# Exchange transfers that write eight spread partitions, bulk loads on the GpSimd queue, and a tile for each exchanged array

## The chip, the cores and the metric

One core of one Trainium2 chip runs the whole program. The metric is the device time of one execution in microseconds (us). The engines of the core are TensorE (PE in the profile, with its weight loads as PEld), VectorE (DVE), ScalarE (ACT), GpSimd (POOL) and SyncE (SP). Transfers are issued from the SP, ACT and POOL queues and run on 16 DMA engines.

## The reference

Two layers of a spectral filter and an MLP over an array x of 2048 rows by 576 columns, in bf16. Each layer has these two residual steps:

```
def _A_ref(x, w_r, w_i):                       # 2-D filter over rows and columns
    X = rfft2(x.astype(float32))               # 2048 x 289 complex
    return irfft2(X * (w_r + 1j * w_i), s=(S, D)).astype(bfloat16)

def _B_ref(x, w1, b1, w2, b2):                 # MLP, 576 -> 4608 -> 576
    y = _layernorm(x)
    h = _gelu(einsum("bsd,df->bsf", y, w1) + b1)
    return einsum("bsf,fd->bsd", h, w2) + b2

x = x + _A_ref(_layernorm(x), w_r, w_i);  x = x + _B_ref(_layernorm(x), ...)   # twice
```

## The kernel before, in words

x stays in SBUF as 16 tiles of 128 rows (x_sb). The Fourier transforms are matrix products on TensorE. The transform along the 2048 rows is split into a step of 16 and a step of 128, and between the two the data must change partitions. An "exchange" does that: a transfer from SBUF to SBUF, 128 rows of 1160 bytes (145 KB), from the SP queue.

A layer runs through these stages:

- SpectralIn (L250 to L322): for each of 16 tiles t, in the order of E_ORDER, fold and layernorm statistics on DVE (L257, L232 to L248; the inverse square root is three Newton steps on DVE, L244 to L247), transposes and two products on PE (L270 to L298), evacuations on ACT or DVE, and an exchange of tile y1 (three buffers, L299) into vx (L304). In the first layer this runs alone (run_all, L309); in the second layer it is woven into the MLP of the first, and only the last tile stands alone after it.
- middle (L327 to L376): 16 steps, each with four matmuls (dft_u, L340), an ACT copy (L342), four DVE operations with the filter weights (L351 to L354), four matmuls (idft_c, L363), an ACT copy into h (three buffers, L365) and an exchange of h into hx (L366). Every dft_u reads all 128 partitions of vx, so the first one needs all 16 exchanges of SpectralIn.
- spectral_out (L380 to L442): products with hx (L391, L404) and c_gd (L420), residual sums on DVE (L426 to L428), and the layernorm of the first quarter for the MLP (Prep, L444). Its first matmul, L404, needs all 16 exchanges of the middle.
- mlp (L516): four quarters of 4 tiles, mlp_up (L472, 38 us) and mlp_down (L497).

Order. Inside a manual_schedule region (L179) every engine, SP too, issues its instructions in the order of the program text. The SP queue carries the x loads, all exchanges, the loads of the first middle (c_f2, filter weights, i1: each exchange of the first SpectralIn is followed by two of them, L305) and those for the MLP (w1 and small ones: one after each exchange of the first middle, L367). The POOL queue carries the w2 loads (L222) and the middle loads of the second layer (L577), which wait until the last mlp_down has read the hidden activations that lie in the same memory.

Memory. One tile, arena_sb, holds vx or hx, w2, the temporaries of the middle and the hidden activations, at offsets. An exchange writes `dst[8 * slot : 8 * slot + 8]`: eight neighbouring partitions.

Of the kernel before, what the change touches and what calls it, by code (L numbers as in the profile page):

```python
# [29 lines left out]
ENGINES = [getattr(mybir.EngineType, n) for n in ("PE", "Activation", "DVE", "Pool", "SP")]  # L30
# [78 lines left out]
def kernel(  # L109
# [40 lines left out]
    arena_sb = arena.tile([P, (OFF_HT + 36864) // 2], BF16, name="arena_sb")  # L150

    def at(shape, name, off):
        n = int(np.prod(shape[1:]))
# [32 lines left out]
    nc.scalar.dma_start(out=c_k1[:], in_=const_ap("k1"))  # L186
    for b in u2r_buf:
        nc.gpsimd.memset(b[:], 0.0)

# [4 lines left out]

    def middle_loads(wks, i1s, with_f2):
        calls = []
        for j in range(4):
            if with_f2:
                calls.append(lambda eng, j=j: eng.dma_start(out=c_f2[:, j::4], in_=f2_ap[:, j::4]))
            for ri, w_ap in enumerate((A_w_r, A_w_i)):  # L200
                wv = w_ap.rearrange("(c e) k -> c e k", e=16)
# [4 lines left out]
    def mlp_const_loads():
        calls = [
            lambda eng: eng.dma_start(out=c_r1[:], in_=const_ap("r1")),
            lambda eng: eng.dma_start(out=c_gd[:], in_=const_ap("gd")),
            lambda eng: eng.dma_start(out=b1_rows[:], in_=B_b1.rearrange("(fc p) -> fc p", p=128)),  # L210
            lambda eng: eng.dma_start(out=b2_bc[:], in_=B_b2.partition_broadcast(P)),
        ]
        for ci in range(4):
            calls.append(lambda eng, ci=ci: eng.dma_start(out=w1_sb[:, ci, :], in_=B_w1[ci * 128 : (ci + 1) * 128, :]))
# [4 lines left out]

    def load_w2(w2s, groups):  # L220
        for g in groups:
            nc.gpsimd.dma_start(  # L222
                out=w2s[g][:], in_=B_w2[g * 768 : (g + 1) * 768, :].rearrange("(fc p) d -> p fc d", p=128)
            )

    def ln_stats(tiles, mlp):
# [100 lines left out]
    def middle(li, vx, hx, wks, i1s, loads):  # L327
        off = OFF_W2 + 18592
        m = {}
        for nm in ("xs", "ma", "mb", "xp"):  # L330
            m[nm] = [(off + 1184 * (len(m) * 2 + b)) for b in range(2)]
        m["h"] = [off + 1184 * (8 + b) for b in range(3)]
        st = {}

        def dft_u(n):
# [180 lines left out]
    def mlp(li, w2s, prep, spec):  # L516
        prev = None
        last = li == N_LAYERS - 1
        for q in range(4):
# [3 lines left out]
            for i, t in enumerate(QUADS[q]):  # L523
# [24 lines left out]

    vx = at([P, 16, 2, KP], "vx", OFF_W2)
    hx = at([P, 16, 2, KP], "hx", OFF_B)  # L550
    wks, i1s = middle_tiles(0)
    for wk in wks:
        nc.gpsimd.memset(wk[:, :, :, KP - 1 : KP], 0.0)
    SpectralIn(vx, middle_loads(wks, i1s, True)).run_all()

    for li in range(N_LAYERS):
        last = li == N_LAYERS - 1
# [8 lines left out]
        spectral_out(hx, prep)
        load_w2(w2s, (0, 1, 2))
        if last:
            mlp(li, w2s, prep, None)
        else:  # L570
            vx = at([P, 16, 2, KP], "vx", OFF_B)
            mlp(li, w2s, prep, SpectralIn(vx))
            hx = at([P, 16, 2, KP], "hx", OFF_W2)
            wks, i1s = middle_tiles(li + 1)
            for wk in wks:
                nc.gpsimd.memset(wk[:, :, :, KP - 1 : KP], 0.0)
            for call in middle_loads(wks, i1s, False):  # L577
                call(nc.gpsimd)
# [30 lines left out]
```

## Time and profile before

| | |
|---|---|
| median of 6 runs | 905.94 us (903.46 to 908.84) |
| the profiled execution's own time | 903.79 us |
| its span, first to last instruction | 902.0 us |
| PE busy | 772.1 us (86%) |
| ACT busy | 330.7 us (37%) |
| DVE busy | 289.3 us (32%) |
| POOL busy | 20.7 us (2%) |
| on the chain that ended last: PE, DMA, DVE | 71%, 16%, 7% |
| moved by DMA | 41.60 MB, mean 46 GB/s |

The shares are means over stages with different limits. The stages, by the start of their first matmul in the trace, are: SpectralIn 1 to 83.2 us, middle 1 to 150.1, spectral_out 1 to 185.5, MLP 1 with SpectralIn 2 to 509 (the end of the last y1 evacuation), a gap to 520.6, middle 2 to 570.3, spectral_out 2 to 605.5, MLP 2 to the end.

### The profile page before, as it was taken

The numbers are of one execution on the slowest core, as the hardware profiler recorded it, in microseconds if no ns is written. First come the engines' busy times: TensorE is split into PE (matmuls) and PEld (weight loads), VectorE is DVE, ScalarE is ACT, GpSimd is POOL, SyncE is SP. The second block draws the span as 40 slices with busy tenths as digits, with TensorE's granted clock in tenths as the row PEclk, the third lists the DMA queues.
The fourth block names the chain that finished last, engine by engine and source line by source line (L and its number), as shares of the span: only waits on it lengthen the run. The fifth ranks groups of instructions, "written<-read, shape, count | busy, mean of one in ns | idle before, by whom it ended". The sixth has DMA issues, their size and how long they took to land.

```text
span 902.0 us, 12359 instructions
## 1 busy us (share of the span) xinstructions
PE 772.1 (86%) x5121; PEld 471.1 (52%) x5121; DVE 289.3 (32%) x989; ACT 330.7 (37%) x506; POOL 20.7 (2%) x38
## 2 busy tenths in 40 slices
PE   5765434799999999999999364689999999999998
PEld 3443222544863684487368232453684485386366
DVE  6632421960442245034014253493013014011001
ACT  3444322356225424632642143336404513521620
POOL 0000001000000000000000400010000000000000
PEclk9997755899999999999999786789999999999999
DMA  6973985300000000000000945330000000000000
GB/s 180 172 132 42 174 158 115 117 0 1 8 14 1 7 15 8 1 14 15 1 7 14 217 51 55 91 118 1 7 15 7 1 15 14 1 14 15 1 7 21
DMA packets 29001, 41.60 MB, mean 46 GB/s; under 512 B 4144, under 2 KB 25072, under 8 KB 28432
## 3 DMA queue, kind: packets, MB, share of 16 engines
q1 hardware_dynamic: 24960, 25.78, 16.3%
q0 software_dynamic: 3584, 14.56, 5.4%
q8 instruction: 40, 0.66, 0.3%
q10 hardware_dynamic: 400, 0.47, 0.2%
q14 instruction: 17, 0.14, 0.1%
HBM read 28.93 MB, written 2.36 MB: 35 GB/s over the span
## 4 chain that ended last, share of the span: by engine, by line
PE 71%; DMA 16%; DVE 7%; ACT 2%; issue 1%; ACTq 0%; DVEq 0%
DMA arena_sb<-arena_sb 11%; DVE tt L426 2%; DMA arena_sb<-y_413 1%; DMA arena_sb<-y_539 1%; DMA arena_sb<-y_4639 1%; DVE x_sb L427 1%; PE psb_4090 L504 1%; PE psb_3278 L504 1%; PE psb_2466 L504 1%; PE psb_7434 L504 1%; PE psb_6818 L504 1%; PE psb_6202 L504 1%; PE psb_5586 L504 1%; PE psb_1704 L504 1%; PE psb_4468 L504 1%
## 5 line engine op out<-in xcount | busy, mean ns | idle before, releaser
L504 PEld LDWEIGHTS <-arena_sb 128*128 128x128 bf16 x2304 | 223.2, 98 | 58.3 <-issue 3.4
L478 PEld LDWEIGHTS <-w_sb 128*128 128x128 bf16 x1152 | 107.3, 98 | 148.7 <-issue 28.1
L456 DVE TENSOR_SCALAR xn<-x_sb,mv,rs 128x576 bf16<-128x576 bf16 x32 | 13.6, 426 | 194.9 <-PE pss_6291 L466 33.8
L232 DVE BATCH_NORM_STATS2 stats<-x_sb 128x6 f32<-128x288 bf16 x128 | 50.4, 436 | 0.0
L340 PEld LDWEIGHTS <-c_f_75 128*128 128x128 bf16 x128 | 15.4, 122 | 64.1 <-issue 45.4
L351 DVE TENSOR_TENSOR arena_sb<-arena_sb 128x580 bf16<-128x580 bf16 x32 | 14.7, 459 | 67.8 <-ACT arena_sb L342 56.7
L280 PEld LDWEIGHTS <-xT 96*128 96x128 bf16 x192 | 21.9, 118 | 14.2 <-ACT xT L272 4.9
L270 PEld LDWEIGHTS <-xf 128*96 128x96 bf16 x192 | 19.2, 159 | 18.0 <-DVE xf L257 16.5
L484 PEld LDWEIGHTS <-w1r_sb 64*128 64x128 bf16 x288 | 8.2, 94 | 30.5 <-issue 30.5
L500 DVE TENSOR_TENSOR xb<-x_sb,b_bc 128x576 f32<-128x576 bf16 x32 | 24.0, 749 | 0.0
L363 PEld LDWEIGHTS <-arena_sb 128*128 128x128 bf16 x128 | 14.3, 119 | 17.4 <-DVE arena_sb L353 6.8
L404 PEld LDWEIGHTS <-arena_sb 128*34 128x34 bf16 x128 | 4.3, 108 | 25.8 <-DMA arena_sb<-arena_sb 24.7
L390 PEld LDWEIGHTS <-arena_sb 128*128 128x128 bf16 x128 | 14.1, 117 | 4.3 <-issue 0.4
L246 DVE TENSOR_TENSOR tt<-tt,hv 128x1 f32<-128x1 f32 (+1 forms) x93 | 14.9, 161 | 3.2
L247 DVE SCALAR_TENSOR_TENSOR rs<-tt,rs 128x1 f32<-128x1 f32 (+1 forms) x93 | 14.9, 160 | 3.2
L245 DVE TENSOR_TENSOR tt<-rs 128x1 f32<-128x1 f32 (+1 forms) x93 | 14.9, 160 | 3.2
L222 POOL DMA_DIRECT2D arena_sb<-in_B_w_dram x12 | 10.0, 840 | 239.6 <-DMA arena_sb<-arena_sb 212.0
L512 DVE TENSOR_TENSOR x_sb<-psb_7434,xb 128x576 bf16<-128x576 f32 x1 | 0.8, 758 | 44.3 <-PE psb_7434 L504 44.3
L352 DVE TENSOR_TENSOR arena_sb<-arena_sb 128x580 bf16<-128x580 bf16 x32 | 14.5, 454 | 0.0
L512 DVE TENSOR_TENSOR x_sb<-psb_4090,xb 128x576 bf16<-128x576 f32 x1 | 0.8, 757 | 42.3 <-PE psb_4090 L504 42.3
L233 DVE BATCH_NORM_AGGREGATE mv<-stats 128x2 f32<-128x12 f32 x64 | 13.4, 209 | 2.2
L466 PEld LDWEIGHTS <-xn 128*128 128x128 bf16 x160 | 11.8, 100 | 3.1 <-DVE xn L456 1.6
(1228 smaller groups left out, 1412.0 us busy)
## 6 DMA issues: line engine op xcount, KB each, us to landing
arena_sb<-in_B_w_dram POOLq DMA_DIRECT2D x12, 864.0 KB, 7.2
arena_sb<-arena_sb SPq DMA_DIRECT2D x32, 145.0 KB
w_sb<-in_B_w_dram SPq DMA_DIRECT2D x4, 1152.0 KB
x_sb<-in_A_x_dram SPq DMA_DIRECT2D x4, 576.0 KB
out_dram<-x_sb SPq DMA_DIRECT2D x16, 144.0 KB
c_f_75<-const_f SPq DMA_DIRECT2D x4, 384.0 KB
arena_sb<-const_i SPq DMA_DIRECT2D x4, 384.0 KB
arena_sb<-const_i POOLq DMA_DIRECT2D x4, 384.0 KB, 9.0
```

Source lines behind the costliest of these rows:

```text
L232: nc.vector.bn_stats(out=stats[:, h, :], in_=x_sb[:, t, h * DH : (h + 1) * DH])
L245: nc.vector.tensor_mul(out=tt[:], in0=rs[:], in1=rs[:])
L246: nc.vector.tensor_mul(out=tt[:], in0=tt[:], in1=hv[:])
L247: nc.vector.scalar_tensor_tensor(out=rs[:], in0=tt[:], scalar=1.5, in1=rs[:], op0=ALU.add, op1=ALU.mult)
L270: nc.tensor.transpose(pt[0:96, 3 * o + ci, :], xf[:, o, 96 * ci : 96 * ci + 96], ident[:])
L280: nc.tensor.matmul(pz[:, o, 0:KP], lhsT=xT[:, 3 * o + ci, :], rhs=c_fd[:, 3 * o + ci, :], start=(ci == 0), stop=(ci == 2),)
L340: nc.tensor.matmul(px[:, o, 0:KP], lhsT=c_f2[:, e, pl, :], rhs=vx[:, e, ri, :], start=(q == 0), stop=(q == 1))
L351: nc.vector.tensor_mul(out=ma[:], in0=xs[:], in1=wr)
L426: nc.vector.tensor_tensor(out=tt[:], in0=po[:, 0:1, 0:DH].to_broadcast([P, 2, DH]), in1=xr, op=ALU.add)
L478: nc.tensor.matmul(phs[q // 2][:, q % 2, :], lhsT=w1_sb[:, ci, (fg + q) * 128 : (fg + q + 1) * 128], rhs=yT[:, ci, :], start=(ci == 0), st ...
L500: nc.vector.tensor_tensor(out=xb[:], in0=xr, in1=b2_bc[:].rearrange("p (h n) -> p h n", h=2), op=ALU.add)
L504: nc.tensor.matmul(po[:, h, 0:DH], lhsT=hts[fc][:, i * 128 : (i + 1) * 128], rhs=w2s[fc // 6][:, fc % 6, h * DH : (h + 1) * DH], start=(fc ...
```

## The change

- An exchange into slot s writes partitions p0, p0+4, ..., p0+28, with p0 = 32 (s // 4) + s % 4, where it wrote 8s to 8s+7. The rows of two constant matrices (f2, r1) are permuted on the host to match (SLOT_ROWS).
- For each pair of exchanges into the same array any ordering that the framework would draw between them is taken away (declare_no_dep).
- SP is no longer among the engines that keep the program's order.
- Bulk loads go to the POOL queue and are issued at the start: three quarters of x, the constants and filter weights of the first middle, then those for the MLP with w1. SP keeps the four first tiles of x, the exchanges and the output.
- arena_sb is cut into v_sb and b_sb (vx and hx by turns), r_sb (temporaries of the middle) and h_sb (hidden activations, or filter weights and i1). w2 comes in 4 parts of 8, 8, 10 and 10 chunks, in v_sb and r_sb, where it came in 6 parts of 6. In layer 1 all four are issued behind the middle; in layer 2 parts 2 and 3 behind the middle and parts 0 and 1 behind spectral_out.
- h has four buffers instead of three.
- In the first SpectralIn and the first Prep the inverse square root is one ACT Sqrt and one DVE reciprocal.
- Two memsets (u2r_buf) move from POOL to DVE.

The core of the diff:

```diff
-ENGINES = [getattr(mybir.EngineType, n) for n in ("PE", "Activation", "DVE", "Pool", "SP")]
+SLOT_ROWS = [8 * (4 * (p // 32) + p % 4) + (p // 4) % 8 for p in range(128)]
+ENGINES = [getattr(mybir.EngineType, n) for n in ("PE", "Activation", "DVE", "Pool")]
...
-    arena_sb = arena.tile([P, (OFF_HT + 36864) // 2], BF16, name="arena_sb")
+    v_sb = arena.tile([P, 9296], BF16, name="v_sb")
+    b_sb = arena.tile([P, 9296], BF16, name="b_sb")
+    r_sb = arena.tile([P, 20 * D], BF16, name="r_sb")
+    h_sb = arena.tile([P, NFC * 512], BF16, name="h_sb")
...
-    for j in range(4):
-        nc.sync.dma_start(out=x_sb[:, j::4, :], in_=xv[:, j::4, :])
+    for t in QUADS[0]:
+        nc.sync.dma_start(out=x_sb[:, t, :], in_=xv[:, t, :])
...
-        nc.gpsimd.memset(b[:], 0.0)
+        nc.vector.memset(b[:], 0.0)
+    for j in range(1, 4):
+        nc.gpsimd.dma_start(out=x_sb[:, j::4, :], in_=xv[:, j::4, :])
...
+    w2_parts = [at(v_sb, [P, 8, D]), at(v_sb, [P, 8, D], 8 * D), at(r_sb, [P, 10, D]), at(r_sb, [P, 10, D], 10 * D)]
+    w2_first = (0, 8, 16, 26, 36)
...
+        if sqrt:
+            sq = work.tile([P, n], F32, tag="ln_v")
+            nc.scalar.activation(out=sq[:], in_=mv[:, :, 1], func=ACT.Sqrt, ...)
+            nc.vector.reciprocal(out=rs[:], in_=sq[:])
+            return [(mv[:, i, 0:1], rs[:, i : i + 1]) for i in range(n)]
...
-            exchange(self.vx, t, y1)
-            for call in self.loads[:2]:
-                call(nc.sync)
-            self.loads = self.loads[2:]
+            exchange(self.vx, t, y1[:])
...
     def exchange(dst, slot, src):
-        nc.sync.dma_start(out=dst[8 * slot : 8 * slot + 8], in_=src[:])
+        p0 = 32 * (slot // 4) + slot % 4
+        ins = nc.sync.dma_start(out=dst[p0 : p0 + 29 : 4], in_=src).ins
+        before = exchanged.setdefault(id(dst), [])
+        for b in before:
+            tc.declare_no_dep(ins, b, query=mybir.DependencyQuery.ANY_SYNC, reason="other partitions of the array")
+        before.append(ins)
...
-            h = at([P, 2, KP], f"h{li}", m["h"][n % 3])
+            h = at(r_sb, [P, 2, KP], 592 * (8 + n % 4))
             nc.scalar.copy(out=h[:], in_=ph[:, :, 0:KP])
             exchange(hx, E_ORDER[n], h)
-            if loads:
-                loads.pop(0)(nc.sync)
...
-    SpectralIn(vx, middle_loads(wks, i1s, True)).run_all()
+    middle_loads(wks, i1s, True)
+    mlp_const_loads()
+    SpectralIn(vx, sqrt=True).run_all()
...
-        load_w2(w2s, (5, 4, 3))
-        prep = Prep(0)
         if li == 0:
+            load_w2((0, 1, 2, 3))
...
+        else:
+            load_w2((2, 3))
+        prep = Prep(0, sqrt=li == 0)
         spectral_out(hx, prep)
-        load_w2(w2s, (0, 1, 2))
         if last:
-            mlp(li, w2s, prep, None)
+            load_w2((0, 1))
+            mlp(li, prep, None)
```

## Rows read from the trace of the kernel before

**Rows 1.** The page's slices: 40 equal parts of the span, DMA busy tenths and GB/s.
```profile
DMA  6973985300000000000000945330000000000000
GB/s 180 172 132 42 174 158 115 117 0 1 8 14 1 7 15 8 1 14 15 1 7 14 217 51 55 91 118 1 7 15 7 1 15 14 1 14 15 1 7 21
```

**Rows 2.** Windows: stretch, length, busy us by engine; PE clock, DMA share, GB/s.
```profile
0.00:10.00 10.00, 1.84 (x11) 1.26 (x12) 2.78 (x14) 2.08 (x2) 2.23 (x11) 1.00 0.80 247
...
186.00:225.00 39.00, 38.36 (x195) 15.56 (x193) 10.17 (x37) 22.62 (x37) 0.00 (x0) 1.00 0.00 1
...
497.00:509.00 12.00, 7.78 (x58) 5.31 (x56) 4.03 (x18) 3.36 (x5) 9.72 (x13) 0.89 0.91 206
509.00:514.00 5.00, 0.00 (x0) 0.00 (x0) 0.00 (x0) 0.55 (x1) 0.00 (x0) 0.50 1.01 289
...
528.00:562.00 34.00, 18.77 (x92) 10.57 (x90) 16.19 (x49) 13.60 (x23) 0.00 (x0) 0.73 0.56 56
```

**Rows 3.** Waits of all engines: who waited for whom, us in total, times, longest.
```profile
ACT arena_sb L365 <- DMA arena_sb<-arena_sb: 58.0, 25, 5.9
```

**Rows 4.** Timeline, borders of the middles: start, us, instruction, idle before.
```profile
83.21 1.12 PE L340 MATMUL psb_763<-arena_sb,c_f_75 128*128 128x290 bf16 x4 [7.35 <-DMA arena_sb<-y_760]
...
150.07 1.04 PE L404 MATMUL pss_1051<-c_r_76,arena_sb 128*34 128x128 bf16 x16 [11.95 <-DMA arena_sb<-arena_sb]
...
509.58 0.61 SPq L325 DMA_DIRECT2D arena_sb<-y_4639  x1
520.64 1.15 PE L340 MATMUL psb_4658<-arena_sb,c_f_75 128*128 128x290 bf16 x4 [11.77 <-DMA arena_sb<-y_4639]
521.59 1.17 PE L340 MATMUL psb_4668<-arena_sb,c_f_75 128*128 128x290 bf16 x4
...
525.25 39.55 SPq L325 DMA_DIRECT2D arena_sb<-arena_sb  x16
...
570.26 1.04 PE L404 MATMUL pss_4933<-c_r_76,arena_sb 128*34 128x128 bf16 x16 [12.12 <-DMA arena_sb<-arena_sb]
```

**Rows 5.** Chain that ended last, the first exchange of middle 2: start, us.
```profile
525.25 5.00 DMA arena_sb<-arena_sb
```

**Rows 6.** Timeline of middle 1, two steps before any exchange is waited for.
```profile
89.11 0.45 DVE L351 TENSOR_TENSOR arena_sb<-arena_sb 128x580 bf16<-128x580 bf16 x1
...
90.48 0.46 DVE L351 TENSOR_TENSOR arena_sb<-arena_sb 128x580 bf16<-128x580 bf16 x1
```

**Rows 7.** Timeline, POOL's bulk loads and SP's exchange in the gap before middle 2.
```profile
497.12 0.76 POOL L202 DMA_DIRECT2D arena_sb<-in_A_w_r_dram  x1 [0.34 <-POOL arena_sb L576]
...
501.38 0.61 SPq L325 DMA_DIRECT2D arena_sb<-y_4576  x1
...
505.99 0.84 POOL L222 DMA_DIRECT2D arena_sb<-in_B_w_dram  x1
```

**Rows 8.** The page's DMA queue of POOL: packets, MB, share of 16 engines.
```profile
q0 software_dynamic: 3584, 14.56, 5.4%
```

**Rows 9.** Timeline of SpectralIn 1: one matmul of neighbouring tiles, early, late.
```profile
11.68 0.40 PE L295 MATMUL psb_199<-z,c_k_74 128*128 128x290 bf16 x1
...
15.28 0.40 PE L295 MATMUL psb_251<-z,c_k_74 128*128 128x290 bf16 x1
...
18.50 0.78 SPq L325 DMA_DIRECT2D arena_sb<-y_204  x1
...
69.96 0.28 PE L295 MATMUL psb_712<-z,c_k_74 128*128 128x290 bf16 x1 [0.42 <-ACT z L285]
...
72.58 0.28 PE L295 MATMUL psb_738<-z,c_k_74 128*128 128x290 bf16 x1 [0.72 <-ACT z L285]
```

**Rows 10.** Groups by line: a Newton operation of the layernorm; and an ACT table load.
```profile
L246 DVE TENSOR_TENSOR tt<-tt,hv 128x1 f32<-128x1 f32 (+1 forms) x93 | 14.9, 161 | 3.2
...
189.48 1.28 ACT L491 ACT_TABLE_LOAD   x1 [5.21 <-PE psb_1468 L484]
```

More of the change, by code (lines that the diff above doesn't have):

```diff
@@ L190, in middle_tiles @@
-    def middle_tiles(li):
-        wks = [at([P, 4, 2, 296], f"wk{li}", OFF_HT + j * 4736) for j in range(4)]
-        i1s = [at([P, 4, 3, P], f"i1_{li}", OFF_HT + 4 * 4736 + j * 3072) for j in range(4)]
+        nc.vector.memset(b[:], 0.0)
+    for j in range(1, 4):
+        nc.gpsimd.dma_start(out=x_sb[:, j::4, :], in_=xv[:, j::4, :])
+    def middle_tiles():
+        wks = [at(h_sb, [P, 4, 2, 296], j * 2368) for j in range(4)]
+        i1s = [at(h_sb, [P, 4, 3, P], 4 * 2368 + j * 1536) for j in range(4)]
+        for wk in wks:
+            nc.gpsimd.memset(wk[:, :, :, KP - 1 : KP], 0.0)
@@ L204, in middle_loads @@
-        return calls
+                nc.gpsimd.dma_start(out=wks[j][:, :, ri, 0 : KP - 1], in_=wv[:, j::4, :])
+            nc.gpsimd.dma_start(out=i1s[j][:], in_=i1_ap[:, j::4])
     def mlp_const_loads():
[L207 to L212, printed above, removed]
+        nc.gpsimd.dma_start(out=c_r1[:], in_=const_ap("r1"))
@@ L213, in mlp_const_loads @@
+        nc.gpsimd.dma_start(out=c_gd[:], in_=const_ap("gd"))
+        nc.gpsimd.dma_start(out=b1_rows[:], in_=B_b1.rearrange("(fc p) -> fc p", p=128))
+        nc.gpsimd.dma_start(out=b2_bc[:], in_=B_b2.partition_broadcast(P))
         for ci in range(4):
[L214 removed]
+            nc.gpsimd.dma_start(out=w1_sb[:, ci, :], in_=B_w1[ci * 128 : (ci + 1) * 128, :])
         rest = B_w1[512:576, :].rearrange("d (j two p) -> d two j p", two=2, p=128)
@@ L216, in mlp_const_loads @@
         for h in range(2):
-            calls.append(lambda eng, h=h: eng.dma_start(out=w1r_sb[64 * h : 64 * h + 64], in_=rest[:, h]))
-        return calls
-    def load_w2(w2s, groups):
+            nc.gpsimd.dma_start(out=w1r_sb[64 * h : 64 * h + 64], in_=rest[:, h])
+    w2_parts = [at(v_sb, [P, 8, D]), at(v_sb, [P, 8, D], 8 * D), at(r_sb, [P, 10, D]), at(r_sb, [P, 10, D], 10 * D)]
+    w2_first = (0, 8, 16, 26, 36)
+    w2_chunk = [w2_parts[g][:, fc - w2_first[g]] for g in range(4) for fc in range(w2_first[g], w2_first[g + 1])]
@@ L221, in load_w2, with ln_stats @@
+    def load_w2(groups):
         for g in groups:
[L222 to L226, printed above, removed]
+            rows = B_w2[w2_first[g] * 128 : w2_first[g + 1] * 128, :]
+            nc.gpsimd.dma_start(out=w2_parts[g], in_=rows.rearrange("(fc p) d -> p fc d", p=128))
+    def ln_stats(tiles, mlp, sqrt):
         n = len(tiles)
@@ L233, in ln_stats @@
             nc.vector.bn_aggr(out=mv[:, i, :], in_=stats[:])
+        rs = work.tile([P, n], F32, tag="ln_rs", bufs=4)
+        if sqrt:
+            sq = work.tile([P, n], F32, tag="ln_v")
+            nc.scalar.activation(
+                out=sq[:], in_=mv[:, :, 1], func=ACT.Sqrt, bias=c_eps[:, 1:2] if mlp else c_eps[:, 0:1], scale=(1.0 + EPS) if mlp else 1.0
+            )
+            nc.vector.reciprocal(out=rs[:], in_=sq[:])
+            return [(mv[:, i, 0:1], rs[:, i : i + 1]) for i in range(n)]
         vv = work.tile([P, n], F32, tag="ln_v")
@@ L250, with __init__ @@
     class SpectralIn:
-        def __init__(self, vx, loads=()):
-            self.vx, self.st, self.loads = vx, {}, list(loads)
+        def __init__(self, vx, sqrt):
+            self.vx, self.st, self.sqrt = vx, {}, sqrt
         def fold(self, t):
@@ L261, in stats @@
         def stats(self, tiles):
-            for t, (_, rs) in zip(tiles, ln_stats(tiles, mlp=False)):
+            for t, (_, rs) in zip(tiles, ln_stats(tiles, mlp=False, sqrt=self.sqrt)):
                 self.st["rs", t] = rs
@@ L322, in run_all, with middle @@
                         self.stats(order[i : i + 4])
+    exchanged = {}
     def exchange(dst, slot, src):
-        nc.sync.dma_start(out=dst[8 * slot : 8 * slot + 8], in_=src[:])
[L327 to L332, printed above, removed]
+        p0 = 32 * (slot // 4) + slot % 4
[4 more added lines that the diff above has]
+        before.append(ins)
+    def middle(vx, hx, wks, i1s):
         st = {}
@@ L340, in dft_u @@
                     nc.tensor.matmul(px[:, o, 0:KP], lhsT=c_f2[:, e, pl, :], rhs=vx[:, e, ri, :], start=(q == 0), stop=(q == 1))
-            xs = at([P, 2, KP], f"xs{li}", m["xs"][n % 2])
+            xs = at(r_sb, [P, 2, KP], 592 * (n % 2))
             nc.scalar.copy(out=xs[:], in_=px[:, :, 0:KP])
@@ L347, in weigh @@
             xs = st.pop(("xs", n))
-            ma, mb, xp = (at([P, 2, KP], f"{nm}{li}", m[nm][n % 2]) for nm in ("ma", "mb", "xp"))
+            ma, mb, xp = (at(r_sb, [P, 2, KP], 592 * (2 * b + n % 2)) for b in (1, 2, 3))
             wr = wk[:, n % 4, 0:1, 0:KP].to_broadcast([P, 2, KP])
@@ L495, in mlp_up, with mlp_down @@
         return hts
-    def mlp_down(t, i, hts, w2s, store, between):
+    def mlp_down(t, i, hts, store, between):
         xb = work.tile([P, 2, DH], F32, tag="f32w", bufs=3)
@@ L539, in mlp @@
                     slots[4].append(lambda p=p: spec.dft_v(p, on_act=True))
-                mlp_down(t, i, hts, w2s, last, slots)
+                mlp_down(t, i, hts, last, slots)
                 prev = t
@@ L547, in mlp @@
             spec.dft_v(prev, on_act=True)
[L549 to L553, printed above, removed]
-    SpectralIn(vx, middle_loads(wks, i1s, True)).run_all()
+    vx, hx = at(v_sb, [P, 16, 2, KP]), at(b_sb, [P, 16, 2, KP])
+    wks, i1s = middle_tiles()
+    middle_loads(wks, i1s, True)
+    mlp_const_loads()
+    SpectralIn(vx, sqrt=True).run_all()
     for li in range(N_LAYERS):
         last = li == N_LAYERS - 1
-        middle(li, vx, hx, wks, i1s, mlp_const_loads() if li == 0 else [])
-        w2s = [at([P, 6, D], f"w2_{li}", OFF_W2 + g * 6912) for g in range(6)]
-        load_w2(w2s, (5, 4, 3))
-        prep = Prep(0)
+        middle(vx, hx, wks, i1s)
         if li == 0:
+            load_w2((0, 1, 2, 3))
             b1p = sm_ps([P, NFC])
@@ L565 @@
             nc.vector.tensor_copy(out=b1_sb[:], in_=b1p[:])
+        else:
+            load_w2((2, 3))
+        prep = Prep(0, sqrt=li == 0)
         spectral_out(hx, prep)
-        load_w2(w2s, (0, 1, 2))
         if last:
-            mlp(li, w2s, prep, None)
-        else:
[L571 to L578, printed above, removed]
+            load_w2((0, 1))
+            mlp(li, prep, None)
+        else:
+            vx, hx = at(b_sb, [P, 16, 2, KP]), at(v_sb, [P, 16, 2, KP])
+            mlp(li, prep, SpectralIn(vx, sqrt=False))
+            wks, i1s = middle_tiles()
+            middle_loads(wks, i1s, False)
 _INS = ['A_x', 'A_w_r', 'A_w_i', 'B_x', 'B_w1', 'B_b1', 'B_w2', 'B_b2']
```

35 lines of the change are left out of this document (14 added, 21 removed).

## The prediction

> **What bounds the kernel now.** I read the slices first: most of the span moves next to nothing by DMA, while two stretches, the first 185 us and about 500 to 605 us, move tens to 180 GB/s [rows 1]. Then windows of single stages. Inside an MLP PE is busy 38.36 of 39 us and DMA share is 0.00 [rows 2]: MLP time is PE's, and the change does nothing there. So only the two spectral stretches can move. In the list of waits, the copy of h in the middle (L365) waits 58.0 us in all for exchanges to have read their buffer [rows 3], and the stage borders in the timeline show who ends each wait: the first dft_u and the first L404 of both layers start when an exchange has landed [rows 4].
>
> The stages that matter, from the starts in [rows 4]: SpectralIn 1 ends at 83.21; middle 1 takes 150.07 - 83.21 = 66.9; the last exchange of SpectralIn 2 is issued at 509.58 and PE goes on at 520.64, a gap of 11.1; middle 2 takes 570.26 - 520.64 = 49.6. Middle 2 has no bulk transfer beside it, so it shows the exchange alone: 16 issues in 39.55 us, (39.55 - 0.61) / 15 = 2.60 us from one to the next, 145 KB at 56 GB/s, with a DMA share of 0.56, about 8 of 16 engines busy [rows 2, 4]. The first, issued at 525.25, releases its buffer 5.00 us later [rows 5]: 2.6 of transfer and 2.4 that do not depend on size. Without such waits a step takes 1.37 us, the interval of L351 on DVE [rows 6]. So the middle is paced by the exchange at twice its own step. Middle 1 is worse because w1 lies between its exchanges on the same queue.
>
> **Part 1: eight spread partitions.** No row shows an exchange to spread partitions. Bounds for its transfer: 2.6 us, if nothing changes; below, the rate of ordinary loads. In the first 10 us loads with rows of 1152 bytes, nearly the exchange's 1160, run at 247 GB/s over 16 engines, 15.4 GB/s each [rows 2]; 18.6 KB per engine on 8 engines is then 1.2 us. I take 1.2, the row of equal length. A gain below zero (a slower exchange) has no reason: the bytes, their count and the engines stay.
>
> A middle then costs: 525.25 - 520.64 = 4.6 to its first exchange [rows 4], 15 steps of 1.37 = 20.6, and 2.4 + 1.2 = 3.6 until the last has landed, in all 28.8. With 1.2 below 1.37 DVE is late next, not the DMA; the four h buffers cover 4 x 1.37 = 5.5 us against 3.6. Middle 2 saves 49.6 - 28.8 = 20.8. Middle 1 saves 66.9 - 28.8 = 38.1, if the bulk loads are done by then (part 2). At a transfer of 2.0 the pace would be 2.0 and each middle 10 us longer.
>
> [...]
>
> **Part 2: bulk loads on POOL from the start.** By the shapes 13.3 MB are queued there: x 1.8, the first middle's 5.5, w1 and the rest 6.0. At the 289 GB/s of the gap [rows 2] that is 46 us. The nearest rows for an exchange beside POOL's loads are in that gap: two exchanges, issued at 501.38 and 509.58, beside loads from 497.12 on, have landed at 520.64 [rows 4, 7]. That is 32 rows on each of 8 engines in 19.2 - 2.4 = 16.8 us, 0.52 us a row instead of 0.16. With the faster exchange 0.43 is left, 6.9 us per exchange; by strict turns (one packet of POOL's queue, 14.56 MB / 3584 = 4.06 KB [rows 8], 0.22 us at 18 GB/s per engine, then a row) it would be 0.30, 4.9 us. From about 14 us (before: 18.5 [rows 9], now with a smaller first x load and no Newton steps) until the loads are through at about 60, some 7 to 9 exchanges land, and three more wait in y1. The other 4 to 6 tiles go at 2.6 to 3.6 us [rows 9], and 3.6 for the last landing: SpectralIn 1 ends at 76 to 81. I take 79, saving 4.2. The ends: 55, if exchanges pass unhindered and all tiles go at 2.62 (12 + 15 x 2.62 + 3.6); 92, if POOL's loads run at the 206 GB/s of 497 to 509 [rows 2] and last until 78.
>
> [...]
>
> **Part 3: the gap.** POOL's middle loads of layer 2 stay where they are. Behind them 0.88 MB of w2 go away (they now wait for r_sb): 0.88 / 0.289 = 3.0 us; the faster exchange takes off up to 32 x 0.09 = 2.9. The floor is a landing of 3.6 instead of 11.1. I take 7: saves 4 (0 to 7.5).
>
> **Part 4: w2.** Layer 1: all four parts, 5.3 MB, behind the middle; at 289 GB/s 18 us, under spectral_out (35 us) and mlp_up (38 us). Layer 2: the last two, 2.4 MB, 8 us under mlp_up. Nothing; without that cover, 18 and 8. On POOL nothing else is queued behind them.
>
> **Part 5: Sqrt.** A Newton operation is 0.16 us [rows 10] and starts about every 0.19; 11 go per call, 2.1 us of DVE. SpectralIn 1 is bound by part 2, so nothing there; it counts only in the unhindered case. In spectral_out 1 DVE instead waits for ACT, behind its copies, and perhaps a table load of 1.28 [rows 10]: saves 0.5 (-1.5 to 2).
>
> **Part 6: SP's order.** Each exchange still waits for its own copy only; out of turn, one would wait for another's copy, a step of 1.4. Nothing.
>
> **Sum.** 4.2 + 38.1 + 4 + 20.8 + 0.5 = 67.6. The profiled execution took 903.79 us, 902.0 of it span: 836.2. The median of the runs is 2.15 above it, so 838.
>
> **The rivals.**
>
> - A, the exchange passes the bulk loads unhindered. For: y1 has three buffers, and the loads are not on its queue. Against: 0.52 us a row. SpectralIn 1 ends between 55 and 70 (12 + 15 x 3.6 + 3.6): 9 to 24 less, 814 to 829.
> - B, bulk is slower and longer. For: 206 GB/s in 497 to 509. SpectralIn 1 ends at 92: 851.
> [...]
> - D, the spreading does nothing: 2.6 remains. Middles as middle 2 now: 17.3 for middle 1, nothing for middle 2; gap 3, SpectralIn 0: 885.
> - E, slower: the partitions of an exchange now lie between those of the others; if waits between exchanges remain, each is issued when the one before has landed, 2.4 + 1.2 = 3.6 apart. Then a middle takes 4.6 + 16 x 3.6 = 62.2 and SpectralIn 1 ends at 60 + 11 x 3.6 = 100: +16.4 - 4.7 + 12.6 = 24, 930. It decides from 3.04 us apart on, where 43 intervals make up the 130.5 us (23.2 + 62.3 + 45.0) that they have before it costs. Against: the change declares the pairs free.
>
> **How the numbers follow.** Forecast 0.48, A 0.18, B 0.16, C 0.06, D 0.05, E 0.07. Predicted is the forecast, 838. The range takes in A, B and C and the bounds of the gap and of part 5: 812 to 864; left out are D and E, 0.12, and a little of the ends. A difference under 0.3% (2.7 us) can't be told from none. Faster: all but E, 0.93, with E near its point 0.02 within and 0.05 slower.
>
> **What would show it.** Middle 2 of about 29 us with issues 1.4 apart, and no wait of L365 on exchanges; middle 1 the same length; if issues stay 2.6 apart, D, if 3.6, E. SpectralIn 1: y1 copies waiting for exchanges until POOL's loads end, at about 60, then not; no such wait is A, loads until 78 are B. The gap: 7 us. MLP stages unchanged. The prediction is wrong if a middle takes longer than 40 us, or if the first dft_u starts before 70 or after 90.

## The result, and the profile after

The changed kernel takes 835.2 us, the median of 10 runs (832.25 to 837.84), beside 904.93 of 20 runs of the kernel before: a ratio of 0.922, 95% interval 0.921 to 0.924. The forecast was 838.0 in a range of 812 to 864. The profiled execution has a span of 833.5 us, 68.5 less than before.

The page's slices of the changed kernel first, the two views of [rows 1] with the granted clock above them, and the chain by engine:

```profile
PEclk9657979999999999999999698899999999999999
DMA  9951650000000000000001634300000000000000
GB/s 296 350 132 40 181 179 1 1 1 8 15 1 2 15 15 1 8 15 8 1 8 33 187 106 152 114 1 1 17 13 1 8 23 0 1 16 16 1 8 22
...
PE 78%; DVE 10%; DMA 9%; ACT 2%; issue 1%; SPq 0%; DVEq 0%; ACTq 0%
```

DMA's share of the chain that ended last fell from 16% to 9%. The loads now stand in the first three slices at up to 350 GB/s, where the first five of before had 180 at most.

The timeline of the changed kernel at the borders of its stages (start, us, instruction, idle before), which answers to [rows 4]. dft_u is L348 now, the first matmul of spectral_out L410, of mlp_up L484, the exchange L334, the copy of h L373, a w2 load L226:

```profile
74.71 1.12 PE L348 MATMUL psb_698<-v_sb,c_f_78 128*128 128x290 bf16 x4 [3.74 <-DMA v_sb<-y_695]
...
110.21 1.04 PE L410 MATMUL pss_977<-c_r_79,b_sb 128*34 128x128 bf16 x16 [10.58 <-DMA b_sb<-r_sb]
...
143.51 1.89 PE L484 MATMUL psb_1379<-yT_1113,w_sb 128*128 128x512 bf16 x8 [0.42 <-DVE x_sb L434]
...
467.59 0.61 SPq L334 DMA_DIRECT2D b_sb<-y_4550  x1
473.94 1.12 PE L348 MATMUL psb_4569<-b_sb,c_f_78 128*128 128x290 bf16 x4 [7.05 <-DMA b_sb<-y_4550]
...
478.98 21.04 SPq L334 DMA_DIRECT2D v_sb<-r_sb  x16
...
502.45 1.04 PE L410 MATMUL pss_4843<-c_r_79,v_sb 128*34 128x128 bf16 x16 [3.79 <-DMA v_sb<-r_sb]
```

The stages by these borders, in us:

| stage | before | forecast | after | saved |
|---|---|---|---|---|
| SpectralIn 1, to its border | 83.2 | 79 | 74.7 | 8.5 |
| middle 1 | 66.9 | 28.8 | 35.5 | 31.4 |
| spectral_out 1 | 35.4 | 34.9 | 33.3 | 2.1 |
| MLP 1 with SpectralIn 2 | 324.1 | 324.1 | 324.1 | 0 |
| gap | 11.1 | 7 | 6.35 | 4.7 |
| middle 2 | 49.6 | 28.8 | 28.5 | 21.1 |
| the rest | 331.7 | 331.7 | 331.0 | 0.7 |

The saved column adds up to 68.5, the difference of the spans. Middle 2, the gap and the MLP came as forecast. SpectralIn 1 saved twice its term, and middle 1 took 6.7 us more than its own, so that the sum hides two misses.

Windows of the changed kernel (columns as in [rows 2]): the loads at the start, the end of middle 1, and middle 2.

```profile
10.00:20.00 10.00, 7.01 (x50) 4.81 (x49) 8.10 (x28) 5.58 (x9) 6.22 (x10) 0.93 1.05 325
20.00:30.00 10.00, 5.75 (x44) 3.98 (x43) 5.25 (x17) 5.07 (x8) 4.15 (x7) 0.84 1.05 303
30.00:40.00 10.00, 7.13 (x36) 4.83 (x36) 1.81 (x6) 4.58 (x8) 3.35 (x5) 0.50 1.02 382
40.00:50.00 10.00, 4.85 (x30) 3.17 (x29) 5.20 (x17) 1.55 (x2) 0.00 (x0) 0.67 0.86 248
...
93.00:104.00 11.00, 4.83 (x29) 2.40 (x29) 5.63 (x19) 4.34 (x8) 1.78 (x2) 0.84 0.86 238
...
479.00:500.00 21.00, 16.70 (x109) 9.54 (x107) 17.52 (x55) 16.66 (x28) 0.02 (x1) 0.99 0.39 105
```

In middle 2 the DMA engines are 0.39 busy at 105 GB/s, where they were 0.56 busy at 56 [rows 2], and DVE with 17.52 of 21 us is the busiest engine. The exchanges are issued (21.04 - 0.61) / 15 = 1.36 us apart, DVE's step, and no wait of L373 for an exchange is left there. The last one is issued at 478.98 + 21.04 - 0.61 = 499.41 and lets L410 start 3.04 us later.

In middle 1, DMA takes a share of 0.86 between 93 and 104 us. The timeline shows with what:

```profile
93.25 0.89 POOL L226 DMA_DIRECT2D v_sb<-in_B_w_dram  x1 [56.41 <-DMA b_sb<-r_sb]
...
96.00 0.89 POOL L226 DMA_DIRECT2D v_sb<-in_B_w_dram  x1 [1.86 <-PE psb_939 L348]
...
105.66 0.64 ACT L373 CAST r_sb<-psb_963 128x580 bf16<-128x580 f32 x1 [7.02 <-DMA b_sb<-r_sb]
```

Parts 0 and 1 of w2 go into v_sb. In the first layer v_sb is vx, which dft_u reads; the second of the loads was let go by a dft_u (L348), not by the end of the middle. The row of the first names an exchange, but the dft_u that reads the last of part 0's memory ended at 92.95, 0.3 us before it, and the second load starts 0.3 us after the end of the last dft_u too. So both run while the last exchanges are under way, and the last copy of h waits 7.02 us for a buffer.

The waits of the changed kernel in SpectralIn 1 (total, times, longest), and its chain there (start, us):

```profile
DVE y_486 L312 <- DMA v_sb<-y_378: 9.3, 1, 9.3
ACT y_515 L310 <- DMA v_sb<-y_428: 9.2, 1, 9.2
DVE y_349 L312 <- DMA v_sb<-y_241: 4.9, 1, 4.9
```

```profile
10.88 9.58 DMA v_sb<-y_203
...
21.20 12.48 DMA v_sb<-y_320
...
34.55 18.02 DMA v_sb<-y_428
...
71.68 2.79 DMA v_sb<-y_695
```

While the loads run, the copies of y1 wait for exchanges, and three exchanges make 40 us of the chain. These are the first, the fourth and the seventh exchange. They land at 20.5, 33.7 and 52.6, so that landings are 4.4 us apart on average (13.2 / 3), later 6.3 (18.9 / 3), where exchanges follow each other every 1.36 us in middle 2. The last exchange of SpectralIn 1, which has no load and no other exchange beside it, takes 2.79 us on the chain; before, the first of middle 2 took 5.00 [rows 5].

### The profile page after: what moved, and what is told of

It is laid out like the page before. It is cut to its first block, busy times and chain, and to the rows that moved or that the text cites. A ratio compares the mean times of both kernels' runs of the same rounds, so it can differ in the third digit from the quotient of the medians.

```text
span 833.5 us, 12285 instructions
## 1 busy us (share of the span) xinstructions
PE 752.5 (90%) x5121; PEld 462.2 (55%) x5121; DVE 275.4 (33%) x905; ACT 331.5 (40%) x514; POOL 37.6 (5%) x61
## 3 DMA queue, kind: packets, MB, share of 16 engines
HBM read 28.93 MB, written 2.36 MB: 38 GB/s over the span
## 4 chain that ended last, share of the span: by engine, by line
PE 78%; DVE 10%; DMA 9%; ACT 2%; issue 1%; SPq 0%; DVEq 0%; ACTq 0%
DMA v_sb<-y_428 2%; DMA b_sb<-r_sb 2%; DVE tt L432 2%; DMA v_sb<-y_320 1%; DVE r_sb L359 1%; DVE r_sb L360 1%; DMA v_sb<-y_203 1%; DVE x_sb L433 1%; PE psb_4001 L510 1%; PE psb_2377 L510 1%; PE psb_3189 L510 1%; PE psb_6727 L510 1%; PE psb_6111 L510 1%; PE psb_5495 L510 1%; PE psb_1615 L510 1%; PE psb_7343 L510 1%
## 5 line engine op out<-in xcount | busy, mean ns | idle before, releaser
L510 PEld LDWEIGHTS <-h_sb 128*128 128x128 bf16 x2304 | 223.1, 98 | 58.2 <-issue 3.4
L484 PEld LDWEIGHTS <-w_sb 128*128 128x128 bf16 x1152 | 107.2, 98 | 148.9 <-issue 28.8
L234 DVE BATCH_NORM_STATS2 stats<-x_sb 128x6 f32<-128x288 bf16 x128 | 50.5, 436 | 0.0
L506 DVE TENSOR_TENSOR xb<-x_sb,b_bc 128x576 f32<-128x576 bf16 x32 | 24.0, 749 | 0.0
L348 PEld LDWEIGHTS <-c_f_78 128*128 128x128 bf16 x128 | 13.8, 109 | 17.0 <-issue 11.8
L371 PEld LDWEIGHTS <-h_sb 128*128 128x128 bf16 x128 | 10.8, 100 | 19.2 <-DVE r_sb L361 10.5
L359 DVE TENSOR_TENSOR r_sb<-r_sb,h_sb 128x580 bf16<-128x580 bf16 x32 | 14.6, 456 | 19.2 <-ACT r_sb L350 19.0
L360 DVE TENSOR_TENSOR r_sb<-r_sb,h_sb 128x580 bf16<-128x580 bf16 x32 | 14.5, 454 | 0.0
L255 DVE TENSOR_TENSOR tt<-tt,hv 128x1 f32<-128x1 f32 (+1 forms) x69 | 11.1, 160 | 2.4
L254 DVE TENSOR_TENSOR tt<-rs 128x1 f32<-128x1 f32 (+1 forms) x69 | 11.1, 160 | 2.4
L256 DVE SCALAR_TENSOR_TENSOR rs<-tt,rs 128x1 f32<-128x1 f32 (+1 forms) x69 | 11.1, 160 | 2.4
L361 DVE TENSOR_TENSOR r_sb<-r_sb 128x290 bf16<-128x290 bf16 x32 | 10.0, 312 | 3.1
## 6 DMA issues: line engine op xcount, KB each, us to landing
w_sb<-in_B_w_dram POOLq DMA_DIRECT2D x4, 1152.0 KB, 14.1
```

The costliest lines, as they stand in the source:

```text
L348: nc.tensor.matmul(px[:, o, 0:KP], lhsT=c_f2[:, e, pl, :], rhs=vx[:, e, ri, :], start=(q == 0), stop=(q == 1))
L359: nc.vector.tensor_mul(out=ma[:], in0=xs[:], in1=wr)
L360: nc.vector.tensor_mul(out=mb[:], in0=xs[:], in1=wi)
L484: nc.tensor.matmul(phs[q // 2][:, q % 2, :], lhsT=w1_sb[:, ci, (fg + q) * 128 : (fg + q + 1) * 128], rhs=yT[:, ci, :], start=(ci == 0), st ...
L506: nc.vector.tensor_tensor(out=xb[:], in0=xr, in1=b2_bc[:].rearrange("p (h n) -> p h n", h=2), op=ALU.add)
L510: nc.tensor.matmul(po[:, h, 0:DH], lhsT=hts[fc][:, i * 128 : (i + 1) * 128], rhs=w2_chunk[fc][:, h * DH : (h + 1) * DH], start=(fc == 0), ...
```

## The experiments

Each kernel differs from the changed kernel by the diff shown. Times are medians beside runs of the kernel before on the same chip, and ratios are to that.

**Do the spread partitions make the exchange faster?**

```diff
-        p0 = 32 * (slot // 4) + slot % 4
-        ins = nc.sync.dma_start(out=dst[p0 : p0 + 29 : 4], in_=src).ins
+        p0 = 8 * slot
+        ins = nc.sync.dma_start(out=dst[p0 : p0 + 8], in_=src).ins
```

SLOT_ROWS follows (here it is the identity). The rest of the change stays.

> The changed kernel with one part undone: an exchange writes eight neighbouring partitions again (own tiles, loads on GpSimd, four h buffers stay). Theory (the spread partitions carry the gain of the middles): exchanges 2.6 us apart again in middle 2, which takes about 49.6 us instead of 28.5; middle 1 about 50 to 55 instead of 35.5; SpectralIn 1 a few us longer, as each exchange holds the engines longer: 835 + 21 + 17 + 5 = 872 to 886. Rival (own tiles, the queue for the loads or the fourth h buffer carry it): 835, middle 2 at 28.5.

Measured: 891.62 us, ratio 0.985 (0.980 to 0.989), 56 more than the changed kernel. Its timeline in middle 2, and a wait:

```profile
512.09 36.01 SPq L334 DMA_DIRECT2D v_sb<-r_sb  x16
...
557.53 1.04 PE L410 MATMUL pss<-c_r,v_sb 128*34 128x128 bf16 x16 [14.73 <-DMA v_sb<-r_sb]
```

```profile
ACT r_sb L373 <- DMA v_sb<-r_sb: 18.1, 12, 2.3
```

The issues are 2.36 us apart, L373 waits again, 12 times, and the last issue, at 547.49, lies 10 us before L410: middle 2 takes 50.5 us from its first dft_u at 507.04. From the first issue to L410 that is 45.4 us, where the kernel before took 45.0 (570.26 - 525.25) [rows 4]: 16 exchanges take as long as before the change. The rest of the change without the spreading (own tiles, the other queue, the fourth h buffer, Sqrt) brings 1.5% of the 7.8%. SpectralIn 1 ends at 86.2 and middle 1 takes 54.0. The time lies above the expectation of 872 to 886, mostly because SpectralIn 1 lost 11.5 us where 5 were expected.

Two variants keep eight spread partitions and change only how they lie. The theory for 16 apart, a transfer between those of 4 apart and of neighbours, was the author's and not shown by any run before. First 16 apart over the whole array:

```diff
-        p0 = 32 * (slot // 4) + slot % 4
-        ins = nc.sync.dma_start(out=dst[p0 : p0 + 29 : 4], in_=src).ins
+        p0 = slot
+        ins = nc.sync.dma_start(out=dst[p0 : p0 + 113 : 16], in_=src).ins
```

> The changed kernel with the eight partitions of an exchange 16 apart instead of 4 apart. [...] Rival (it is only the distance between the partitions that counts): as the changed kernel in every row, share 0.39. Total 835 to 842 by the theory, 835 by the rival.

Measured: 841.07 us, ratio 0.928 (0.925 to 0.930). Then 2 apart, within 16 neighbouring partitions, where the author expected what 16 apart had shown, 838 to 844 us:

```diff
-        p0 = 32 * (slot // 4) + slot % 4
-        ins = nc.sync.dma_start(out=dst[p0 : p0 + 29 : 4], in_=src).ins
+        p0 = 16 * (slot // 2) + slot % 2
+        ins = nc.sync.dma_start(out=dst[p0 : p0 + 15 : 2], in_=src).ins
```

> The changed kernel with the eight partitions of an exchange 2 apart, so that they lie within 16 neighbouring ones; with them 16 apart over the whole array the time was 841.07 us, SpectralIn 1 ended at 80.73 and the last landing of middle 2 took 3.62 us against 3.04. [...]

Measured: 844.81 us, ratio 0.934 (0.930 to 0.937). Middle 2 of the two, 16 apart and then 2 apart:

```profile
485.43 20.74 SPq L334 DMA_DIRECT2D v_sb<-r_sb  x16
...
509.18 1.04 PE L410 MATMUL pss<-c_r,v_sb 128*34 128x128 bf16 x16 [4.36 <-DMA v_sb<-r_sb]
```

```profile
486.34 21.23 SPq L334 DMA_DIRECT2D v_sb<-r_sb  x16
...
511.69 1.04 PE L410 MATMUL pss<-c_r,v_sb 128*34 128x128 bf16 x16 [5.96 <-DMA v_sb<-r_sb]
```

The last landing of middle 2 takes 3.04 us at 4 apart, 3.62 at 16 apart (485.43 + 20.74 - 0.61 = 505.56, to 509.18), and 4.73 at 2 apart (506.96 to 511.69); in the kernels below that have own tiles, all at 4 apart, it is 2.84 to 3.11. So 2 apart did not land as 16 apart does, and its time missed what was expected by 0.8 us; its issues are 1.37 us apart ((21.23 - 0.61) / 15), those of 16 apart 1.34 ((20.74 - 0.61) / 15). But in middle 2 one exchange follows another. The last exchange of SpectralIn 1 stands alone (nearly so with neighbours), and the chains show it for 16 apart, 2 apart and neighbours, in this order, beside 2.79 us at 4 apart:

```profile
77.17 3.32 DMA v_sb<-y
```

```profile
74.53 3.35 DMA v_sb<-y
```

```profile
80.93 5.02 DMA v_sb<-y
```

Alone, the two variants take the same. In middle 2, L373 waits for exchanges 4 times at 2 apart, and the list of waits has none at 16 apart: at 2 apart some exchanges are late for the next copy, and the last one may have landed behind others. The order of the four lone exchanges is 2.79 at 4 apart, then 3.32 and 3.35 at 16 and 2 apart, then 5.02 for neighbours. A rule by the distance between partitions alone would not put 16 apart behind 4 apart; what makes the order, the runs do not show. Why 16 apart keeps to DVE's step under load and 2 apart does not is open too. The DMA share at 16 apart is 0.42 from 486 to 506, beside 0.39 at 4 apart.

**What is the spreading alone worth?** To the kernel before, with its one arena_sb, its queues and its order, only the partitions of the exchange and SLOT_ROWS are changed; no pair is declared free:

```diff
-        nc.sync.dma_start(out=dst[8 * slot : 8 * slot + 8], in_=src[:])
+        p0 = 32 * (slot // 4) + slot % 4
+        nc.sync.dma_start(out=dst[p0 : p0 + 29 : 4], in_=src[:])
```

> The kernel before with the spread partitions alone: one arena, loads on SP, SP in the program's order, three h buffers, Newton steps. Here the framework draws a wait of each exchange for the one before it, as the strided target overlaps its neighbours' span in the one arena. [...] Rival (spreading alone carries the gain): issues 1.4 apart, middle 2 at 28.5, total under 880.

Measured: 1064.77 us, ratio 1.176 (1.172 to 1.180): slower than before, by 160 us. The author had put it at 905 to 935, with issues of middle 2 a landing of 3.0 to 3.6 us apart. From its timeline in middle 2 (dft_u is L342 here), and its waits:

```profile
643.70 83.48 SPq L327 DMA_DIRECT2D arena_sb<-arena_sb  x16
...
652.16 1.15 PE L342 MATMUL psb<-arena_sb,c_f 128*128 128x290 bf16 x4 [3.51 <-DMA arena_sb<-arena_sb]
...
657.81 1.15 PE L342 MATMUL psb<-arena_sb,c_f 128*128 128x290 bf16 x4 [3.54 <-DMA arena_sb<-arena_sb]
```

```profile
PE psb L342 <- DMA arena_sb<-arena_sb: 102.0, 26, 11.2
PE psb L506 <- DMA arena_sb<-y: 53.2, 15, 3.6
```

dft_u reads vx and the exchange writes hx, yet each dft_u waits for the exchange of the step before. mlp_down (L506) reads the hidden activations and waits for an exchange of y1. So an exchange with spread partitions in the one tile is ordered against readers of other data in that tile as well, and not only against other exchanges. A step is then its computation plus a landing, 5.65 us. Of the 160 us middle 2 lost 53 and MLP 1, with the second SpectralIn in it, 77. The transfer itself did get faster, as the chain shows for the first exchange of middle 2, which took 5.00 before [rows 5]:

```profile
643.70 2.78 DMA arena_sb<-arena_sb
```

**Do the declarations do anything?** They are taken away:

```diff
-        before = exchanged.setdefault(id(dst), [])
-        for b in before:
-            tc.declare_no_dep(ins, b, query=mybir.DependencyQuery.ANY_SYNC, reason="other partitions of the array")
-        before.append(ins)
```

> The changed kernel without the declarations that take waits between exchanges away; each array still has its own tile. Theory (with own tiles the framework draws no such wait, and the declarations change nothing): middle 2 at 28.5 us with issues 1.4 apart, total 835. Rival (the declarations are what keeps the exchanges from waiting): middle 2 at 54 us or more, total above 880.

Measured: 838.28 us in one run, middle 2 28.45 us. Its timeline there:

```profile
482.16 20.96 SPq L334 DMA_DIRECT2D v_sb<-r_sb  x16
```

The issues are 1.36 apart. The own tiles do what is needed, and the declarations bring nothing that shows. SpectralIn 1 ends at 77.68 in this run, 3.0 us later than in the changed kernel. Its PE was granted 0.50 between 60 and 70 us, where the changed kernel had 0.84; here first the changed kernel, then this one:

```profile
60.00:70.00 10.00, 7.14 (x51) 4.82 (x50) 1.96 (x4) 6.19 (x8) 0.00 (x0) 0.84 0.17 46
```

```profile
60.00:70.00 10.00, 8.80 (x46) 6.10 (x45) 1.20 (x3) 5.40 (x8) 0.00 (x0) 0.50 0.17 46
```

**What is the move to POOL worth?** The loads go back to SP, in the places that they had before, with SP in the order of the program; the spreading and the own tiles stay, and the declarations are left out:

```diff
+            for _ in range(2):
+                if queue:
+                    queue.pop(0)(nc.sync)
...
-                nc.gpsimd.dma_start(out=c_f2[:, j::4], in_=f2_ap[:, j::4])
+                calls.append(lambda eng, j=j: eng.dma_start(out=c_f2[:, j::4], in_=f2_ap[:, j::4]))
```

> The changed kernel with one part undone: the loads of x, of the first middle and of the MLP go through SP between the exchanges again, in the program's order, as in the kernel before; own tiles and spread partitions stay. Theory (the queue itself saves little, the engines are shared anyway): SpectralIn 1 at 68 to 76 us, middle 1 at 36 to 46 because w1 lies between its exchanges, middle 2 at 28.5; total 833 to 848. Rival (the GpSimd queue is a main part of the gain): middle 1 above 55, total above 855.

Measured: 838.82 us, ratio 0.927 (0.924 to 0.930), 3.6 more than the changed kernel. Its borders (dft_u is L350, L410 is L414 here), and a wait:

```profile
59.97 2.34 PE L350 MATMUL psb<-v_sb,c_f 128*128 128x290 bf16 x9 [3.73 <-DMA v_sb<-y]
...
112.81 1.04 PE L414 MATMUL pss<-c_r,b_sb 128*34 128x128 bf16 x16 [10.66 <-DMA b_sb<-r_sb]
```

```profile
ACT r_sb L375 <- DMA b_sb<-r_sb: 27.3, 9, 7.8
```

SpectralIn 1 ends 14.7 us earlier than in the changed kernel, middle 1 takes 52.8 and so 17.3 longer. Both lie outside the expectation (68 to 76; 36 to 46), and they nearly cancel: middle 1 ends 2.6 us later. In both kernels the loads pass within the first 113 us, and the queue decides which exchanges they meet. Middle 2 takes 28.4 us here, though SP keeps the program's order and no pair is declared free: neither of them is what held the exchanges up in the one arena_sb.

**What do w2 and w1 cost beside exchanges?** In layer 1 the w2 parts that go into r_sb come first; they can't start before the middle's last buffers are read:

```diff
-            load_w2((0, 1, 2, 3))
+            load_w2((2, 3, 0, 1))
```

> The changed kernel with the four w2 loads of layer 1 in the order 2, 3, 0, 1, so that POOL first waits for the end of middle 1 and parts 0 and 1 no longer start at 93 us, when the last dft_u has read v_sb. Theory (these two loads stand in the way of the last four or five exchanges of middle 1): middle 1 takes 28.5 to 29.5 us instead of 35.5, as middle 2 does, total 828 to 829. Rival (middle 1 is longer for another reason): 835, middle 1 at 35.5.

Measured: 828.76 us, ratio 0.915 (0.911 to 0.918). Then w1 as well, behind the first of these parts (w1_loads holds the loads of w1, cut out of those at the start):

```diff
-            load_w2((0, 1, 2, 3))
+            load_w2((2,))
+            w1_loads()
+            load_w2((3, 0, 1))
```

> The changed kernel with w1 loaded behind middle 1 (w2 part 2 first, which waits for it, then w1, then w2 parts 3, 0, 1), instead of during SpectralIn 1. Theory (the exchanges of SpectralIn 1 wait for their turn beside the bulk loads): 5.3 MB less beside them, loads end at about 30 instead of 47, the two waits of 9 us for exchanges at 35 to 52 go, SpectralIn 1 ends at 58 to 64 instead of 74.7; middle 1 28.5 to 29.5; w1 has landed by 25 us before the MLP needs it: total 812 to 819. Rival (SpectralIn 1 is bound by its own PE and ACT work at the low clock): it ends at 70 to 75, total 826 to 829.

Measured: 816.67 us, ratio 0.901 (0.898 to 0.904), faster than both kernels. The borders of the first of the two:

```profile
75.00 3.06 PE L348 MATMUL psb<-v_sb,c_f 128*128 128x290 bf16 x12 [3.78 <-DMA v_sb<-y]
...
80.04 21.14 SPq L334 DMA_DIRECT2D b_sb<-r_sb  x16
...
103.60 1.04 PE L410 MATMUL pss<-c_r,b_sb 128*34 128x128 bf16 x16 [3.66 <-DMA b_sb<-r_sb]
```

And of the second (L350 and L412 here):

```profile
60.63 1.61 PE L350 MATMUL psb<-v_sb,c_f 128*128 128x290 bf16 x6 [3.74 <-DMA v_sb<-y]
...
87.70 2.11 POOL L216 DMA_DIRECT2D w_sb<-in_B_w_dram  x4
89.04 1.04 PE L412 MATMUL pss<-c_r,b_sb 128*34 128x128 bf16 x16 [3.65 <-DMA b_sb<-r_sb]
```

With w2 out of the way middle 1 is 28.6 us, as long as middle 2: the 6.7 us by which it missed its forecast were that collision. With w1 out of the way SpectralIn 1 ends 14.1 us earlier. w1 then comes under spectral_out 1, and costs nothing there: mlp_up starts 33.2 us after L412, where it took 33.3 in the changed kernel.

**What is the Sqrt worth?** Newton steps again, first in the changed kernel, then in the kernel with w1 behind the middle:

```diff
-    SpectralIn(vx, sqrt=True).run_all()
+    SpectralIn(vx, sqrt=False).run_all()
...
-        prep = Prep(0, sqrt=li == 0)
+        prep = Prep(0)
```

> The changed kernel with the three Newton steps in place of ACT's square root everywhere. Theory (in spectral_out 1 DVE is the bound, so its 2.1 us of small operations are on the path): spectral_out 1 takes 35.4 us instead of 33.3, SpectralIn 1 changes by less than 2, total 836 to 839. Rival (the wait for ACT eats it): 835, spectral_out 1 at 33.3.

Measured: 844.93 us, ratio 0.932 (0.929 to 0.936), 9.7 more than with Sqrt, 9.0 of it in SpectralIn 1 of the profiled execution. Neither theory had that. The border, and two windows:

```profile
83.74 1.61 PE L348 MATMUL psb<-v_sb,c_f 128*128 128x290 bf16 x6 [3.76 <-DMA v_sb<-y]
```

```profile
50.00:60.00 10.00, 6.18 (x32) 4.30 (x32) 5.24 (x17) 4.56 (x7) 0.00 (x0) 0.50 0.29 73
60.00:70.00 10.00, 8.74 (x44) 5.79 (x43) 4.33 (x19) 4.99 (x7) 0.00 (x0) 0.50 0.18 47
```

> The kernel with w1 loaded behind middle 1 (816.67 us, SpectralIn 1 to 60.63), without Sqrt: Newton steps on DVE everywhere. Without Sqrt the changed kernel was 9.7 us slower, 9.0 of it in SpectralIn 1, and its PE had a granted clock of 0.50 from 50 to 84 us. Theory 1 (the Newton steps delay each tile on DVE's own queue): the 9.0 stays, SpectralIn 1 ends at 68 to 72, and spectral_out 1 adds 2.8: 826 to 830 us. Theory 2 (most of the 9 came with the slow clock, and from the exchanges beside w1, which fell otherwise): SpectralIn 1 ends at 60 to 65, time 818 to 823 us.

Measured: 819.19 us, ratio 0.906 (0.902 to 0.911), 2.5 more than with Sqrt, though the times overlap (817.69 to 827.35 and 813.59 to 819.54). Its border, and the window of 50 to 60:

```profile
63.65 3.06 PE L350 MATMUL psb<-v_sb,c_f 128*128 128x290 bf16 x12 [3.75 <-DMA v_sb<-y]
```

```profile
50.00:60.00 10.00, 6.93 (x55) 4.26 (x53) 2.88 (x9) 6.36 (x10) 0.00 (x0) 1.00 0.25 67
```

Here SpectralIn 1 loses 3.0 us, not 9.0, as the second theory had it, and spectral_out 1 takes 35.2 where it took 33.2. So about 6 of the 9 us in SpectralIn 1 came only with w1 beside it. In that kernel PE is granted 0.50 in both windows and does the tiles behind the loads at that rate; here it is 1.00. The kernel without the declarations tells a part of this: it has Sqrt and the same loads, was granted 0.50 from 60 to 70 us too, and ends SpectralIn 1 at 77.68, 3.0 us behind the changed kernel without any Newton step and 6.1 ahead of the kernel with them. So about 3 of the 9.0 us can go with the clock alone. How the other 6 divide between the Newton steps and the exchanges that fell beside w1 these runs don't separate, and each border is that of one execution.

## Why the prediction was right, and where not

- **Part 1, spread partitions: right.** Middle 2 was to take 28.8 and took 28.5, with DVE's step as its pace. The landing was put at 3.6 and is 3.04, or 2.79 on the chain, the view from which the 5.00 of before comes. With the estimate of 2.4 beside the transfer (5.00 - 2.60) kept, 0.4 to 0.6 is left for the transfer: less than the 1.2 from the loads of 0 to 10 us. Rival D fell with the changed kernel's own pace of 1.36, and the kernel with neighbours, where issues are 2.36 us apart and the 45 us to L410 came back, shows that the partitions made it. These runs vary nothing but the partitions, and do not show what in the hardware makes the difference.
- **Middle 1: the mechanism right, a collision missed.** The step that failed is in part 4, "all four parts, 5.3 MB, behind the middle", priced at nothing. They stand there in the program, but POOL waits for memory, not for the middle. Two parts write vx, which is free when the last dft_u has read it. With the order 2, 3, 0, 1 the forecast of 28.8 came true (28.6).
- **Part 2, SpectralIn 1: a term mis-sized, 8.5 for 4.2.** From 10 to 40 us the DMA engines moved 303 to 382 GB/s, exchanges included, not 289. The last load was issued at 35.97 and landed 18.8 us later, so that the loads were through at about 55 us instead of 60, and most of them by 46, where the share falls from 1.03 (40 to 46) to 0.60 (46 to 50). The exchanges beside them landed 4.4 to 6.3 us apart, near the 4.9 to 6.9 of the estimate. Behind them the tiles came 3.1 us apart (issues from 53.34 to 71.68, 18.3 / 6), within the 2.6 to 3.6 of the prediction. With these terms its sum allows 74.0 (60 + 4 x 2.6 + 3.6) to 85.2 (60 + 6 x 3.6 + 3.6), wider than the 76 to 81 that it gives. The expected mark, copies of y1 waiting for exchanges until the loads end, is there; rival A is excluded for this order of loads, and so is B, the slower loads, which needed 206 GB/s.
- **Part 5, Sqrt: "SpectralIn 1 is bound by part 2, so nothing there" failed.** Without it SpectralIn 1 ends 9.0 us later in the profiled executions, at 83.74 (83.21 in the kernel before). About 3 of the 9.0 can be the clock; what the rest is made of stays open. In spectral_out 1 the term was 0.5 and the runs show 2.0 to 2.8. What the queue is worth can't be read from the 83.74, since w1 and spread exchanges are in it; the kernel with the loads on SP is nearer to a test, and there the queue brought 2.6 us by the end of middle 1.
- **Part 3, the gap: right.** 6.35 for 7.
- **Part 6: right**, as far as the trace shows: no exchange on SP held up a later one in the middles.
- **Rival C**, the case of a lower granted clock in the middles, did not come: the clock in middle 2 is 0.99, where it was 0.73 [rows 2]; PE is busy 16.70 of 21 us there, and was 18.77 of 34.
- **Rival E** was the right danger at the wrong price. It was put at 3.6 us between exchanges and 930 us; in one tile it is 5.65 a step and 1064.77, because readers of other data are held too. What keeps it away here is the own tiles: without the declarations, and with SP in order too, no such wait appears. The prediction's reason, "the change declares the pairs free", was not what mattered.

That the predicted time came within 3 us is in part luck: SpectralIn 1 gave 4.3 us more, spectral_out 1 1.6, the gap 0.7, the rest 0.7 and middle 2 0.3, while middle 1 took 6.7 back.

## What to carry to other kernels

When one transfer repeats at a fixed rate with half of the DMA engines busy, as middle 2 of before did (2.60 us apart at a share of 0.56), look at which partitions it writes before its size or its queue, and give its target a tile of its own before spreading it. A load that stands behind a stage in the program can start inside it, as w2 did at 93.25 and 96.00, with 17 and 14 us of middle 1 to go: follow each target to its last reader, and see what transfers are still under way then. Moving the bulk loads to another queue chose here which stage pays (SpectralIn 1 14.7 us longer, middle 1 17.3 shorter); put them beside a stage that has no exchanges of its own, here spectral_out 1, which took 33.2 us with w1 beside it and 33.3 in the changed kernel.

## What was not expected of the hardware

- Eight partitions 2 apart and eight 16 apart take the same when an exchange stands alone (3.35 and 3.32 us). With an exchange every 1.37 and 1.34 us the last landing differs by 1.1 (4.73 against 3.62).
- With the bulk loads on the POOL queue the DMA engines moved up to 382 GB/s in a stretch of 10 us, where the fastest stretch shown of before was 289 [rows 2].
- With Newton steps SpectralIn 1 ended 9.0 us later beside w1's load and 3.0 later without it, in single executions; about 3 of the 9.0 can be the lower clock (granted 0.50 from 60 to 70 us, where the changed kernel had 0.84).
